# Passing quarter totals and the carry of a lane scan between partitions: small TensorE products or ScalarE copies

## The chip, the cores and the metric

One Trainium2 chip, one core of it. The kernel is one program; its five compute engines are named as in the profile: PE (TensorE, with PEld for its weight loads), DVE (VectorE), ACT (ScalarE), POOL (GpSimd) and SP (SyncE). Data lies in SBUF, which has 128 partitions, and PE writes to eight PSUM banks, here called d0, d1, d2, sc0, sc1, tr0, tr1 and yp. The metric is the time of one execution on the device, in microseconds; lower is better.

## What is computed

A gated linear scan with complex gates (4 batches, 8 heads, 768 tokens, width 48) gives x of 3072 tokens by 384 columns, and a layer pair with squared ReLU follows. Cut to what matters:

```python
mag = np.sqrt(a_re * a_re + a_im * a_im)
scale = np.minimum(mag, 0.999) / (mag + 1e-06)
a_re_n, a_im_n = (a_re * scale, a_im * scale)
for t in range(S):                     # per batch and head, state 48 x 48, complex
    new_re = ar * S_re - ai * S_im     # ar, ai: gate of token t, one per row
    new_im = ar * S_im + ai * S_re
    S_re, S_im = (new_re + outer(k_t, v_t), new_im)
    y[t] = q_t @ S_re
x = y.transpose(0, 2, 1, 3).reshape(3072, 384)
out = np.maximum(x @ w_in, 0) ** 2 @ w_out       # w_in 384 x 2048, w_out 2048 x 384
```

## The kernel before

**Units.** The 3072 tokens are worked off in six units of 512 (n = 0 to 5). A sequence has 768 tokens, so units 0 and 3 begin one ("fresh" is unit 3 in the code of the lane scan), units 1 and 4 have a border between two sequences in their middle ("cross"), and units 2 and 5 are plain. Within a unit the gates are turned into running products, so that the scan becomes matmuls with masks:

- the *chain* (`chain(n)`) takes roots, normalises the gates and forms their running complex product over the 512 tokens;
- `apply` multiplies q and k by it and by its inverse;
- the *pairs* (`pairs(n)`) work on eight pairs of heads: turn (line 1668), score (1689) with the mask on DVE (1692), keep (1717) with the state on DVE or ACT (1731, 1727), and mix (1748, 1752), whose sum ACT copies out of PSUM (1761) and DMAs carry into xT;
- the *dense* part is the layer pair: products of the first layer at line 1799, squared ReLU on ACT (1832, 1833), products of the second layer at line 1847 for unit 0 and at line 1910 for the rest; the last half unit has its own variant at line 2055. Between units, and in the first 130 us, weights are also split into 16-bit parts on ACT and DVE (lines 961 to 975).

**The lane scan.** In units 1 to 5 the running product is formed in `lanes()`. The 128 partitions are four quarters of 32, and within each quarter a lane holds a stretch of tokens. The running product is first formed inside the lanes on DVE (lines 1203 and 1215, with small copies on ACT at 1315). Then the quarters have to learn of each other. `times(dst, x, y, ...)` is one complex product of 128 x 24 numbers: one DVE instruction at line 1327 and two at line 1331. `qx` is the total of each quarter, made by `times` from the totals of two half quarters, h0 and h1. `exchange()` multiplies qx by `shifts`, a matrix 256 wide whose left half repeats the last 32 columns of the identity and whose right half is the identity. A window of it that is moved by 32, 64 or 96 columns gives qx shifted down by one, two or three quarters; where a quarter has no predecessor, it gets the value of the last quarter of qx, which is preset to 1. The results s1, s2, s3 lie in a bank tr0 or tr1. A plain unit then forms few2 = s2 * s3 (one operand is first copied from PSUM at line 1353), car = car * s1 and E0 = car * few2: what all lanes before this quarter have multiplied up to. Cross units need s1 alone.

**The carry.** `ce` is a unit's total at its end, needed by the next unit as `car`. `carry()` copies it from the last quarter to all four by one more product with `shifts` (line 1429) into a tr bank and one ACT copy out of it (line 1431). In cross units only the lower half is used, and POOL presets the upper half of car to 1 (times a scale, SCALE). Unit 1 uses another matrix for this, made by POOL at line 1426, since unit 0 leaves ce in a different layout (four ACT copies at line 1291).

**What sets the order.** All steps are entered in a list by `Plan.add` with engine, estimated duration, dependencies and a rank; `Plan.order()` then simulates the engines and picks the ready step with the lowest rank. `SHIFTS` adds numbers to the ranks of single steps, by their place in the list. `GROUP` is how long (in us) a narrow PE step (score or mix) is held back while another narrow one is about to get ready, so that they stand together. Engines then work off their instructions strictly in the emitted order, and DMAs stand in the queues of the engine that issues them (SP, ACT, POOL).

Of the kernel before, what the change touches and what calls it, by code (L numbers as in the profile page):

```python
# [16 lines left out]
ALU = mybir.AluOpType  # L17
# [464 lines left out]
class Plan:  # L482
# [13 lines left out]
    SHIFTS = {  # L496
        -2392.0: (2058,),
        -1993.0: (2427,),
        -1403.0: (2178,),
        -1100.0: (1860,),  # L500
        -1002.0: (1861,),
        -985.0: (1659,),
        -602.0: (1652,),
        -601.0: (1813,),
        -512.0: (1012,),
        -500.0: (1820,),
        -409.0: (1017,),
        -404.0: (1801,),
        -401.0: (1807, 1815,),
        -301.0: (2275,),  # L510
        -209.0: (541,),
        -202.0: (793, 795, 815, 821, 2276,),
        -197.0: (1818,),
        -104.0: (341,),
        -100.0: (range(109, 112), range(113, 116), 166, 229, 361, 432, 475, range(521, 523), 686,
            837, 940, 949, 982, 1397, 1403, range(1627, 1630), range(1762, 1764), 1806,
            range(1821, 1824), range(1827, 1829), range(2095, 2097), range(2098, 2100),
            range(2101, 2103), range(2104, 2106), 2116, 2163, 2165, 2236, range(2277, 2279),
            2431, 2562, 2581,),
        1.0: (2416, range(2434, 2436), 2444,),  # L520
        100.0: (27, 210, 234, 269, 290, 294, range(296, 298), 304, 306, 314, 327, 329, 386, 395,
            406, 425, 430, 434, 443, 449, 466, 473, 497, range(507, 509), 549, range(568, 570),
            582, 584, 587, 590, range(663, 665), 716, 720, 735, 738, 742, 789, 852, 891, 915,
            920, 925, 944, 961, 1129, range(1180, 1182), 1183, 1247, 1316, 1373, 1385, 1570,
            1719, 1732, 1784, 1798, 1819, 2161, 2174, 2222, 2362, 2382, 2386, 2394, 2437, 2440,
            2443, 2534, 2548, 2623, 2631, 2638, 2654,),
        198.0: (287,),
        202.0: (339,),
        203.0: (2114,),
        294.0: (1273,),  # L530
        297.0: (363,),
        299.0: (289, 808,),
        300.0: (1583,),
        306.0: (1824, 2085,),
        393.0: (585,),
        400.0: (787,),
        410.0: (1696,),
        429.0: (683,),
        496.0: (465,),
        504.0: (832,),  # L540
        506.0: (810,),
        508.0: (514,),
        509.0: (1694,),
        605.0: (535,),
        733.0: (682,),
        796.0: (2355,),
        807.0: (1699,),
        808.0: (1700,),
        906.0: (702,),
        907.0: (731, 737,),  # L550
        908.0: (1693,),
        1001.0: (751,),
        1008.0: (1697,),
        1010.0: (451,),
        1203.0: (753,),
        1317.0: (2536,),
        1320.0: (2567,),
        1505.0: (2031,),
        1515.0: (2591,),
        1614.0: (2600,),  # L560
        1734.0: (421,),
        1997.0: (537,),
        2341.0: (888,),
        2646.0: (894,),
        2969.0: (412,),
        3572.0: (409,),
        3772.0: (408,),
        3776.0: (413,),
        5321.0: (402,),
        9116.0: (36,),  # L570
        9619.0: (414,),
        10027.0: (31,),
        10523.0: (39,),
        10527.0: (410,),
        11514.0: (407,),
    }

    def __init__(self):
# [138 lines left out]
def fast_path(ctx, tc, q, k, v, a_re, a_im, moe_w_in, moe_w_out, out, flag):  # L717
# [6 lines left out]
    C = 128  # L724
# [11 lines left out]
    SCALE = 2.0 ** 59  # L736
# [19 lines left out]
    dve, pool, act, sp = nc.vector, nc.gpsimd, nc.scalar, nc.sync  # L756
    pe = nc.tensor
# [5 lines left out]
    def sb(name, n, dtype=F32, rows=C):  # L763
        return const.tile([rows, n], dtype, name=name)
# [18 lines left out]
    ce, car, qx = [sb(name, 2 * NK).rearrange("p (r k) -> p r k", r=2)  # L783
                   for name in ("ce", "car", "qx")]
# [270 lines left out]
    def chain(n):  # L1055
# [164 lines left out]
        K = kk_(0)  # L1220
# [18 lines left out]
        def scan():  # L1239
# [49 lines left out]
            for x in range(4):  # L1289
                own = slice(32 * x, 32 * x + 32)  # L1290
                step("ACT", 0.13, [("ce0",), ("A", 0)], [("ce",)], lambda x=x, own=own: act.copy(
                    out=ce[own].rearrange("p r (m x) -> p r m x", x=4)[:, :, :, x],
                    in_=ce0[own]), late[0], group="ce")

        def back(j):
# [8 lines left out]
        def lanes():  # L1304
# [27 lines left out]
                             out=dst[0:rows, r], in0=g[:, 0, r], in1=g[:, 1, 1 - r], op=op), rk)  # L1332

            times(qx, h0, h1, i4k, [("qx",)], rows=C - 32)
            if cross:
                def apart():
                    dve.memset(qx[32:64, 0], 1.0)
                    dve.memset(qx[32:64, 1], 0.0)
                step("DVE", 0.14, [], [("qx",)], apart, ahead)
            b = trs[take("tr", 2)]  # L1340
            s1, s2, s3 = [bank[b][:, j * 2 * NK:(j + 1) * 2 * NK].rearrange(
                "p (r k) -> p r k", r=2) for j in range(3)]

            def exchange():
                for j, o in enumerate((s1, s2, s3)[:1 if cross else 3]):
                    x0 = C - 32 * (j + 1)
                    pe.matmul(o, lhsT=shifts[:, x0:x0 + C], rhs=qx, start=True, stop=True)
            step("PE", 0.12 * (1 if cross else 3), [("qx",)], [(b,)], exchange, ahead)
            E0 = tx[:, :, 0:NK]
            two2, few2 = [KC[0][:, i:i + 2 * NK].rearrange("p (r k) -> p r k", r=2)  # L1350
                          for i in (64, 96)]
            if not cross:
                step("DVE", 0.1, [(b,)], [("ev", 0)], lambda: dve.tensor_scalar(
                    out=two2, in0=s2, scalar1=SCALE if fresh else 1.0, scalar2=None,
                    op0=ALU.mult), ahead)
            if cross:
                times(E0, car, s1, [(b,), ("car",)], [("tx", 0)])
            elif fresh:
                times(few2, two2, s3, [(b,), ("ev", 0)], [("ev",)])
                times(E0, s1, few2, [(b,), ("ev",)], [("tx", 0)])  # L1360
            else:
                times(few2, two2, s3, [(b,), ("ev", 0)], [("ev",)])
                times(car, car, s1, [(b,), ("car",)], [("car",)])
                times(E0, car, few2, [("car",), ("ev",)], [("tx", 0)])
            times(tx[:, :, NK:2 * NK], h0, E0, i4k + [("tx", 0)], [("tx", 1)])
            X = [("tx", 0), ("tx", 1)]
# [36 lines left out]
                times(ce, h1, tx[:, :, NK:2 * NK], i4k + X, [("ce",)], at=yts[0][:, 384:512], own="H", rk=late[1])  # L1403

        def carry():
            if fresh:
                return
            b = trs[take("tr", 2)]
            ps = bank[b][:, 0:2 * NK].rearrange("p (r k) -> p r k", r=2)
            rows = C // 2 if cross else C  # L1410

            def go():
                if cross:
                    pool.memset(car[C // 2:C, 0], SCALE)
                    pool.memset(car[C // 2:C, 1], 0.0)
            if cross:
                step("POOL", 0.2, [], [("car",)], go, ahead)

            by = shifts[:, 0:C]
            if n == 1:  # L1420
                by = KC[0][:, 1152:1152 + C]

                def same():
                    for x in range(4):
                        own = slice(32 * x, 32 * x + 32)
                        pool.tensor_copy(out=by[own].rearrange("p (b c) -> p b c", c=32),
                                         in_=ident[own, own].unsqueeze(1).to_broadcast([32, 4, 32]))
                step("POOL", 1.2, [], K, same, ahead)
            step("PE", 0.12, [("ce",)] + K * (n == 1), [(b,)], lambda: pe.matmul(
                ps, lhsT=by, rhs=ce, start=True, stop=True), ahead)  # L1430
            step("ACT", 0.15, [(b,)], [("car",)], lambda: act.copy(
                out=car[0:rows], in_=ps[0:rows]), ahead)

        if n:
            carry()
# [163 lines left out]
    def take(kind, n):  # L1599
        s = slot[kind]  # L1600
        slot[kind] = s + 1
        return s % n
# [615 lines left out]
```

## Time and profile before

| | |
|---|---|
| median of 3 runs | 663.99 us (663.62 to 665.3) |
| profiled execution, its own time | 663.7 us |
| its span, first to last instruction | 661.6 us |
| granted TensorE clock, mean | 0.990 |
| PE busy | 617.8 us (93%), 4424 records |
| PEld busy | 552.2 us (83%) |
| DVE busy | 589.1 us (89%) |
| ACT busy | 341.5 us (52%) |
| POOL busy | 120.6 us (18%) |
| chain that ended last, by engine | PE 70%, DVE 18%, DMA 6%, ACT 3% |

The profiled execution took 0.3 us less than the median, and 2.1 us of its own time lie outside its span. Each float32 matmul of the program shows as two PE records. Busy times of PE are modelled ends of a pipelined engine, so the start of one record against the start of the next tells more than the sum of durations.

### The profile page before, as it was taken

How to read it: one execution, taken by the hardware profiler on the slowest of the kernel's cores; microseconds unless marked ns; L12 is line 12 of the kernel's file. 1: busy time of each engine (PE TensorE's matmuls, PEld its weight loads, DVE VectorE, ACT ScalarE, POOL GpSimd, SP SyncE). 2: the span in 40 equal slices, each digit the busy share in tenths (PEclk: the TensorE clock that was granted, in tenths of full speed). 3: DMA queues.
4: the chain of work that ended last, by engine and by line, in shares of the span. 5: the costliest groups of instructions: out<-in, count | busy, mean ns of one | idle time of the engine just before them, and what ended most of it. 6: DMA issues, size and time to landing. Idle time of an engine off the chain costs nothing.

```text
span 661.6 us, 12065 instructions
## 1 busy us (share of the span) xinstructions
PE 617.8 (93%) x4424; PEld 552.2 (83%) x4424; DVE 589.1 (89%) x1196; ACT 341.5 (52%) x608; POOL 120.6 (18%) x208
## 2 busy tenths in 40 slices
PE   0468899999999999999999999999999999999996
PEld 0356887687679988999989999989989999988996
DVE  7999999899998999998979898989998997449982
ACT  7759979769626245438254447254446532035400
POOL 7402140221100032040121040111030130032100
PEclk9979999999999999999999999999999999999999
DMA  7963676024620056452056562056470063368541
GB/s 225 311 228 73 144 223 184 23 67 133 153 82 1 1 125 157 125 157 37 10 142 165 129 136 45 19 118 174 114 177 0 13 141 95 73 195 277 196 162 29
DMA packets 55269, 80.35 MB, mean 121 GB/s; under 512 B 11393, under 2 KB 37921, under 8 KB 55201
## 3 DMA queue, kind: packets, MB, share of 16 engines
q0 software_dynamic: 15424, 42.12, 22.5%
q1 hardware_dynamic: 35168, 31.93, 19.0%
q10 hardware_dynamic: 4608, 5.44, 3.2%
q8 instruction: 37, 0.61, 0.4%
q14 instruction: 32, 0.25, 0.1%
HBM read 48.76 MB, written 4.72 MB: 81 GB/s over the span
## 4 chain that ended last, share of the span: by engine, by line
PE 70%; DVE 18%; DMA 6%; ACT 3%; issue 2%; ACTq 0%; POOL 0%; DVEq 0%; SPq 0%
PE d L1910 25%; PE d L1799 24%; PE sc L1689 3%; PE yp L1748 3%; DVE f L1489 3%; PE d L1847 3%; DVE f L1554 3%; PE tr L1717 2%; DMA w<-in_moe_w_in_dram 2%; PE yp L1752 2%; PE d L2055 2%; PE tr L2055 2%; DVE aq L1642 1%; PE sc L2055 1%; DVE aq L1506 1%
## 5 line engine op out<-in xcount | busy, mean ns | idle before, releaser
L1799 PE MATMUL d<-xT,w 128*128 128x256 f32 x888 | 200.2, 381 | 0.8 <-DMA xT<-yt 0.5
L1799 PEld LDWEIGHTS d<-xT,w 128*128 128x128 f32 x888 | 166.5, 190 | 23.6 <-ACT g L1832 0.7
L1910 PE MATMUL d<-T,g 128*128 128x192 f32 x576 | 100.2, 329 | 0.0
L1910 PEld LDWEIGHTS d<-T,g 128*128 128x128 f32 x576 | 93.7, 190 | 1.5 <-issue 0.9
L1832 ACT ACTIVATE g<-d 128x512 f32<-128x512 f32 x74 | 44.1, 596 | 77.6 <-PE d L1799 64.6
L1865 POOL DMA_DIRECT2D out_dram<-ot x40 | 25.5, 642 | 277.7 <-DVE ot L1935 223.7
L1910 PE MATMUL d<-w,g 128*128 128x192 f32 x432 | 75.8, 328 | 0.3 <-ACT g L1833 0.3
L1910 PEld LDWEIGHTS d<-w,g 128*128 128x128 f32 x432 | 70.7, 190 | 1.5 <-ACT g L1833 0.6
L1590 POOL DMA_DIRECT2D KC<-f x60 | 32.4, 552 | 121.9 <-DVE f L1554 94.4
L1926 DVE TENSOR_TENSOR g<-g 128x512 f32<-128x512 f32 x72 | 48.5, 688 | 6.4 <-ACT g L1833 3.0
L1833 ACT ACTIVATE g<-g 128x512 f32<-128x512 f32 x80 | 50.5, 631 | 2.5
L1489 DVE TENSOR_TENSOR f<-aq,xn 128x384 f32<-128x384 f32 (+1 forms) x72 | 47.5, 686 | 0.0
L1847 PE MATMUL d<-w,g 128*128 128x384 f32 x128 | 44.2, 491 | 0.0
L1642 DVE STREAM_TRANSPOSE aq<-f 128x384 f32<-128x384 f32 (+1 forms) x51 | 42.1, 902 | 0.2
L1520 ACT ACTIVATE f<-aq 128x768 f32<-128x768 f32 (+1 forms) x16 | 17.3, 1081 | 43.7 <-DVE aq L1506 36.1
L1689 PEld LDWEIGHTS sc<-QT 96*64 96x64 f32 x736 | 33.5, 137 | 5.4 <-ACT QT L1672 2.0
L1689 PE MATMUL sc<-QT 96*64 96x128 f32 (+1 forms) x736 | 35.8, 249 | 1.9 <-DVE A L1692 0.8
L1128 DVE TENSOR_TENSOR f<-aq 128x384 f32<-128x384 f32 x72 | 37.1, 553 | 0.5
L1847 PEld LDWEIGHTS d<-w,g 128*128 128x128 f32 x128 | 23.6, 190 | 13.7 <-issue 0.2
L1935 DVE TENSOR_TENSOR ot<-ot,d 128x192 f32<-128x192 f32 x70 | 23.6, 350 | 10.3 <-PE d L1910 9.7
L1692 DVE TENSOR_TENSOR A<-sc,mask 128x512 f32<-128x512 f32 x45 | 29.6, 683 | 3.0 <-PE sc L1689 3.0
L1748 PE MATMUL yp<-A,v 128*48 128x128 f32 x312 | 29.0, 276 | 0.0
(315 smaller groups left out, 1104.5 us busy)
## 6 DMA issues: line engine op xcount, KB each, us to landing
QT<-aq SPq DMA_DIRECT2D x136, 64.0 KB, 2.1
f<-in_moe_w_in_dram POOLq DMA_DIRECT2D x8, 768.0 KB, 6.8
f<-in_moe_w_out_dram POOLq DMA_DIRECT2D x8, 768.0 KB, 5.3
QT<-aq ACTq DMA_DIRECT2D x68, 64.0 KB, 2.4
KC<-f POOLq DMA_DIRECT2D x40, 96.0 KB, 3.3
out_dram<-ot POOLq DMA_DIRECT2D x40, 96.0 KB, 3.6
xT<-yt SPq DMA_DIRECT2D x34, 96.0 KB, 2.6
T<-in_moe_w_out_dram POOLq DMA_DIRECT2D x4, 768.0 KB, 11.6
```

Source lines behind the costliest of these rows:

```text
L1128: lambda c=c, j=j: dve.tensor_tensor(out=f[:, j], in0=a[:, :, :, c - 1], in1=a[:, j, :, c].unsqueeze(1).to_broadcast([C, 2, HH, D]), op=AL ...
L1489: lambda j=j, r=r: dve.tensor_tensor(out=f4[:, j, r], in0=a[:, r], in1=over(j), op=ALU.mult), rk)
L1642: lambda src=src, dst=dst: dve.transpose(out=dst, in_=src), rank)
L1689: pe.matmul(sa[p0:p0 + CH, j, t0:], lhsT=T[:, j, 1, h, t0:t0 + CH], rhs=T[:, j, 0, h, t0:], start=True, stop=True)
L1748: pe.matmul(ps[64 * h:64 * h + D, j - js[0]], lhsT=v5[:, j, 2 * i + h], rhs=aa[h][:, j], start=True, stop=at[j] is None)
L1799: pe.matmul(ps, lhsT=w1[:, f // FP, m, ts(f % FP, C)], rhs=xT[:, n % 2, m, ts(grp, G)], start=(m == 0), stop=(m == NM - 1))
L1832: act.activation(out=o, in_=ps, func=AF.Relu)
L1833: act.activation(out=o, in_=o, func=AF.Square)
L1847: pe.matmul(ps, lhsT=gt[:, f % 2, ts(i, C)], rhs=w2[:, f], start=(f == 0), stop=(f == NF - 1))
L1910: pe.matmul(bank[b][:, 0:DH], lhsT=gsets[x][h][:, j - HW * h, r], rhs=w(j), start=first and j == 0, stop=last and j == NT - 1)
L1926: lambda: dve.tensor_tensor(out=g[:, :, o], in0=g[:, :, x0], in1=g[:, :, x1], op=op),
L2055: pe.matmul(ps[:, jj], lhsT=u[:, ts(jj, C)], rhs=v_, start=i == 0, stop=i == len(terms) - 1)
```

## The change

1. `exchange()`, its products and its bank go. In their place ACT copies quarters of qx into three SBUF tiles s1, s2, s3, shifted by 32, 64 or 96 partitions: two copies in a cross unit, five in each other unit. The quarters without a predecessor are preset to 1 and 0 once by POOL. DVE's copy out of PSUM (line 1353) and its two memsets of qx in cross units go too.
2. `carry()` has no product either: ACT copies the last quarter of ce to the quarters of car, four copies in units 2 and 5, two in units 1 and 4, none in unit 3. POOL presets what is left of car, in unit 3 all of it; unit 3 then also multiplies car by s1, which it did not before (three more DVE instructions). In cross units POOL also presets one quarter of s1. Unit 0 puts its four parts of ce into the last quarter, so that unit 1 needs no matrix of its own.
3. `shifts` shrinks to its right half, `ident`.
4. GROUP goes from 8 to 4, and the table SHIFTS is replaced as a whole, so that steps change places on every engine.

Counted over the program: 15 products less on PE (11 of exchange, 4 of the carry, 30 records), 31 small copies more on ACT and 4 copies out of PSUM less, 7 small instructions less and 3 more on DVE, some small presets more and fewer on POOL.

```diff
-    SETTLED, GROUP = 90.0, 8
+    SETTLED, GROUP = 90.0, 4
...
     SHIFTS = {
-        -2392.0: (2058,),
...
+        -4734.0: (468,),
...
-    shifts = sb("shifts", 2 * C)
-    ident = shifts[:, C:2 * C]
+    ident = sb("ident", C)
...
-    pool.tensor_copy(out=shifts[:, 0:C].rearrange("p (b c) -> p b c", c=32),
-                     in_=ident[:, C - 32:C].unsqueeze(1).to_broadcast([C, 4, 32]))
-    pool.memset(ce, 0.0)
-    pool.memset(qx[:, 0], 1.0)
-    pool.memset(qx[:, 1], 0.0)
+    for t in sx:
+        pool.memset(t[:, 0], 1.0)
+        pool.memset(t[:, 1], 0.0)
...
             times(qx, h0, h1, i4k, [("qx",)], rows=C - 32)
+            for j in range(1 if cross else 3):
+                for lo in (0, 64) if cross else (0, 32, 64) if j == 0 else (0,):
+                    hi = lo + (64 if j == 1 else 32)
+                    up = slice(lo + 32 * (j + 1), hi + 32 * (j + 1))
+                    step("ACT", 0.13, [("qx",)], [("sx", j)], lambda j=j, lo=lo, hi=hi, up=up: act.copy(
+                        out=sx[j][up], in_=qx[lo:hi]), ahead, group=(n, "sx"))
...
-            b = trs[take("tr", 2)]
-            s1, s2, s3 = [bank[b][:, j * 2 * NK:(j + 1) * 2 * NK].rearrange(
-                "p (r k) -> p r k", r=2) for j in range(3)]
-
-            def exchange():
-                for j, o in enumerate((s1, s2, s3)[:1 if cross else 3]):
-                    x0 = C - 32 * (j + 1)
-                    pe.matmul(o, lhsT=shifts[:, x0:x0 + C], rhs=qx, start=True, stop=True)
-            step("PE", 0.12 * (1 if cross else 3), [("qx",)], [(b,)], exchange, ahead)
...
-            if not cross:
-                step("DVE", 0.1, [(b,)], [("ev", 0)], lambda: dve.tensor_scalar(
-                    out=two2, in0=s2, scalar1=SCALE if fresh else 1.0, scalar2=None,
-                    op0=ALU.mult), ahead)
             if cross:
-                times(E0, car, s1, [(b,), ("car",)], [("tx", 0)])
-            elif fresh:
-                times(few2, two2, s3, [(b,), ("ev", 0)], [("ev",)])
-                times(E0, s1, few2, [(b,), ("ev",)], [("tx", 0)])
+                times(E0, car, sx[0], [("sx", 0), ("car",)], [("tx", 0)])
             else:
-                times(few2, two2, s3, [(b,), ("ev", 0)], [("ev",)])
-                times(car, car, s1, [(b,), ("car",)], [("car",)])
+                times(few2, sx[1], sx[2], [("sx", 1), ("sx", 2)], [("ev",)])
+                times(car, car, sx[0], [("sx", 0), ("car",)], [("car",)])
                 times(E0, car, few2, [("car",), ("ev",)], [("tx", 0)])
...
         def carry():
-            if fresh:
-                return
-            b = trs[take("tr", 2)]
...
-            step("PE", 0.12, [("ce",)] + K * (n == 1), [(b,)], lambda: pe.matmul(
-                ps, lhsT=by, rhs=ce, start=True, stop=True), ahead)
-            step("ACT", 0.15, [(b,)], [("car",)], lambda: act.copy(
-                out=car[0:rows], in_=ps[0:rows]), ahead)
+            rows = 0 if fresh else C // 2 if cross else C
+            if rows < C:
+                def start():
+                    pool.memset(car[rows:C, 0], SCALE)
+                    pool.memset(car[rows:C, 1], 0.0)
+                    if cross:
+                        pool.memset(sx[0][C // 2:C // 2 + 32, 0], 1.0)
+                        pool.memset(sx[0][C // 2:C // 2 + 32, 1], 0.0)
+                step("POOL", 0.4, [], [("car",), ("sx", 0)], start, ahead)
+            for b in range(rows // 32):
+                step("ACT", 0.13, [("ce",)], [("car",)], lambda b=b: act.copy(
+                    out=car[32 * b:32 * b + 32], in_=ce[C - 32:C]), ahead, group=(n, "car"))
```

The places where the order moves under the prediction's steps follow. In the rows a name stands with the number of its buffer; line numbers are those of each kernel's own file, so that 1799 before is 1784 after, 1692 is 1677, 1327 and 1331 are 1343 and 1347, 1832 and 1833 are 1817 and 1818, 968, 972 and 975 are 984, 988 and 991, and 1731 is 1716.

PE before, at the hand-over of unit 2's lane scan, where the first layer of an earlier unit runs:

```order
L1799 MATMUL d0_109<-xT_93,w1_66 128x256 x6
L1799 MATMUL d1_110<-xT_93,w1_66 128x256 x3
L1347 MATMUL tr1_115<-qx_83,shifts_97 128x24 x3
L1799 MATMUL d1_110<-xT_93,w1_66 128x256 x3
L1799 MATMUL sc1_113<-xT_93,w1_66 128x256 x4
```

PE after, at the same place:

```order
L1784 MATMUL sc1_116<-xT_96,w1_66 128x256 x4
L1784 MATMUL d0_112<-xT_96,w1_66 128x256 x6
L1784 MATMUL d1_113<-xT_96,w1_66 128x256 x6
L1784 MATMUL sc0_115<-xT_96,w1_66 128x256 x4
L1784 MATMUL yp_119<-xT_96,w1_66 128x256 x4
```

The three products of qx are gone, and the two halves of the tile d1 stand together.

DVE before, at the hand-over of unit 1 (qx made, preset for the border, then the first use of the shifted totals):

```order
L1327 TENSOR_TENSOR KC0_76<-yt0_91 96x48
L1331 TENSOR_TENSOR qx_83<-KC0_76 96x12 x2
L1337 MEMSET qx_83 32x12
L1338 MEMSET qx_83 32x12
L975 ISA w2_67<-T_72,w2_67 128x1536
L1327 TENSOR_TENSOR KC0_76<-car_82,tr1_115 128x48
```

DVE after, at the same place:

```order
L1343 TENSOR_TENSOR KC0_76<-yt0_94 96x48
L1347 TENSOR_TENSOR qx_83<-KC0_76 96x12 x2
L1343 TENSOR_TENSOR KC0_76<-car_82,s1_84 128x48
L1347 TENSOR_TENSOR tx_80<-KC0_76 128x12 x2
L1343 TENSOR_TENSOR KC0_76<-yt0_94,tx_80 128x48
```

The joining of weight parts that stood between qx and its first use is no longer there; the first reader of the copies comes directly behind qx.

ACT after, at the same hand-over (977 and 982 prepare parts of w_out, 1331 is a small copy inside the lanes, 1355 is the new copy):

```order
L977 ACTIVATE T_72<-T_72 128x768
L1331 COPY yt0_94<-e_79 128x96 x2
L982 ACTIVATE T_72<-T_72 128x768
L1355 COPY s1_84<-qx_83 32x24 x2
L1376 COPY KC0_76<-tx_80 128x2x12
```

The copies of qx stand behind one long preparation of weights (982, which is 966 before).

DVE before, around the last masks of unit 0 (1692), the last scores ahead of the first layer:

```order
L1692 TENSOR_TENSOR A1_88<-sc1_113,mask_98 128x512
L1692 TENSOR_TENSOR A0_87<-sc0_112,mask_98 128x512
L975 ISA w1_66<-g_96,w1_66 128x1536
L968 TENSOR_SCALAR w1_66<-T_72 128x768
L1731 TENSOR_TENSOR St1_90<-tr1_115,St1_90 96x96 x2
L968 TENSOR_SCALAR w1_66<-g_96 128x768
L972 SCALAR_TENSOR_TENSOR w1_66<-g_96,w1_66 128x768
L1692 TENSOR_TENSOR A0_87<-sc0_112,mask_98 128x512
L1692 TENSOR_TENSOR A1_88<-sc1_113,mask_98 128x512
```

DVE after, at the same place:

```order
L988 SCALAR_TENSOR_TENSOR w1_66<-g_99,w1_66 128x768
L1100 TENSOR_TENSOR f0_70<-f0_70 128x768
L991 ISA w1_66<-g_99,w1_66 128x1536
L984 TENSOR_SCALAR w1_66<-w2_67 128x768
L991 ISA w1_66<-w2_67,w1_66 128x1536
L1677 TENSOR_TENSOR A0_90<-sc0_115,mask_101 128x512
L1716 TENSOR_TENSOR St1_93<-tr1_118,St1_93 96x96
L1677 TENSOR_TENSOR A1_91<-sc1_116,mask_101 128x512
```

Other splittings of w_in stand between the masks now, and over the whole of unit 0 three instructions of line 968 that stood ahead of the last mask stand behind it.

More of the change, by code (lines that the diff above doesn't have):

```diff
@@ L515 @@
[L515 to L526, printed above, removed]
@@ L568 @@
[L568 to L575, printed above, removed]
+        -4734.0: (468,),
+        -4118.0: (582,),
+        -4010.0: (1085,),
+        -3812.0: (1083,),
+        -3809.0: (583,),
+        -3735.0: (471,),
+        -3719.0: (580,),
+        -2621.0: (593,),
+        -2610.0: (591,),
+        -2298.0: (816,),
+        -2202.0: (814,),
+        -1816.0: (544,),
@@ new lines @@
+        -1624.0: (1008,),
+        -1419.0: (463,),
+        -1219.0: (1012,),
+        -1207.0: (320,),
+        -1008.0: (946,),
+        -997.0: (466,),
+        -904.0: (1643, 1646,),
+        -898.0: (1133,),
+        -897.0: (592,),
+        -894.0: (562,),
+        -806.0: (1623,),
+        -804.0: (1614, 1620,),
+        -704.0: (1649,),
+        -703.0: (1132,),
+        -698.0: (469,),
+        -697.0: (417,),
+        -678.0: (292,),
+        -605.0: (458,),
+        -603.0: (1617,),
@@ new lines @@
+        107.0: (1720,),
+        194.72: (9,),
+        195.02: (11,),
+        206.0: (1689,),
+        296.0: (2124,),
+        397.0: (854,),
+        398.0: (933,),
+        402.0: (985,),
+        409.0: (1230,),
+        500.0: (930,),
+        591.0: (2157,),
+        603.0: (1419,),
+        609.0: (2377,),
+        610.0: (864,),
+        710.0: (871,),
+        804.0: (1188,),
+        906.0: (1890,),
+        908.0: (856,),
+        1015.0: (870,),
+        1200.0: (1167,),
+        1204.0: (1429,),
@@ L576 @@
+        1406.0: (867,),
+        1605.0: (1185,),
+        1917.0: (438,),
+        2115.0: (868,),
+        2592.0: (2185,),
+        4190.0: (402,),
+        4199.0: (1360,),
+        4296.0: (410,),
+        4487.0: (426,),
+        4892.0: (431,),
+        5820.0: (446,),
+        6733.0: (419,),
+        6932.0: (430,),
+        7038.0: (442,),
     }
@@ L782, in fast_path @@
     tx = sb("tx", 4 * NK).rearrange("p (r g) -> p r g", r=2)
-    ce, car, qx = [sb(name, 2 * NK).rearrange("p (r k) -> p r k", r=2)
-                   for name in ("ce", "car", "qx")]
+    ce, car, qx, *sx = [sb(name, 2 * NK).rearrange("p (r k) -> p r k", r=2)
+                        for name in ("ce", "car", "qx", "s1", "s2", "s3")]
     xn = sb("xn", 2 * DM).rearrange("p (r n) -> p r n", r=2)
@@ L1291, in scan @@
                 step("ACT", 0.13, [("ce0",), ("A", 0)], [("ce",)], lambda x=x, own=own: act.copy(
-                    out=ce[own].rearrange("p r (m x) -> p r m x", x=4)[:, :, :, x],
+                    out=ce[C - 32:C].rearrange("p r (m x) -> p r m x", x=4)[:, :, :, x],
                     in_=ce0[own]), late[0], group="ce")
```

117 lines of the change are left out of this document (34 added, 83 removed).

## The prediction

> **What bounds the kernel now.** I read first the page's shares, then the engine sums by stretch, then PE's waits from the first dense products to the end, and last the neighbourhood of each product that goes. The shares and PE's row of tenths:
>
> ```profile
> PE 617.8 (93%) x4424; PEld 552.2 (83%) x4424; DVE 589.1 (89%) x1196; ACT 341.5 (52%) x608; POOL 120.6 (18%) x208
> PE   0468899999999999999999999999999999999996
> ```
>
> PE and DVE are both near full, so the shares alone don't decide. The sums by stretch (length, then busy time and count of PE, PEld, DVE, ACT, POOL, then clock, DMA share, GB/s):
>
> ```profile
> core 0: us, PE busy (x) PEld busy (x) DVE busy (x) ACT busy (x) POOL busy (x), PEclk, DMA share, GB/s
> 52.00:86.00 34.00, 29.13 (x382) 25.81 (x381) 33.45 (x67) 30.33 (x50) 5.98 (x12) 1.00 0.49 112
> 86.00:260.00 174.00, 173.26 (x1094) 142.65 (x1092) 165.78 (x356) 110.09 (x197) 34.15 (x56) 1.00 0.40 105
> 260.00:656.00 396.00, 394.70 (x2855) 367.15 (x2854) 342.73 (x661) 165.78 (x292) 59.26 (x91) 1.00 0.44 115
> ```
>
> From 86 us on PE lacks 0.74 and 1.30 us; DVE has 8 and 53 us to spare there. PE's waits from 86 to 656 us (total, times, longest):
>
> ```profile
> PE tr L2055 <- DMA xT<-yt: 1.0, 1, 1.0
> PE tr L1429 <- DVE St L1731: 0.5, 1, 0.5
> PE d L1910 <- ACT g L1833: 0.3, 1, 0.3
> PE d L1799 <- ACT g L1832: 0.3, 1, 0.3
> ```
>
> Four waits in 570 us, 2.1 us together. So here PE streams, and what is taken out of its stream should shorten the time by its place in the stream. Ahead of 86 us it is the other way: DVE is busy 33.45 of 34 us, and PE waits for it. What is in doubt is whether a stream that waits for nothing also has work ready that may move up.
>
> **The products that go.** PE records overlap, so I price a product by the start of its first record to the start of PE's next work:
>
> ```profile
> 203.67 2.11 PE L1799 MATMUL d<-xT,w 128*128 128x256 f32 x9
> 205.61 0.74 PE L1347 MATMUL tr<-qx,shifts 128*128 128x24 f32 x6
> 206.20 1.54 PE L1799 MATMUL d<-xT,w 128*128 128x256 f32 x6
> ...
> 402.91 0.30 PE L1347 MATMUL tr<-qx,shifts 128*128 128x24 f32 x2
> 403.05 4.13 PE L1799 MATMUL d<-xT,w 128*128 128x256 f32 x18
> ```
>
> ```profile
> 179.49 0.40 PE L1429 MATMUL tr<-ce,shifts 128*128 128x24 f32 x2 [0.45 <-DVE St L1731]
> 179.74 1.54 PE L1847 MATMUL d<-w,g 128*128 128x384 f32 x4
> ...
> 372.51 0.40 PE L1429 MATMUL tr<-ce,shifts 128*128 128x24 f32 x2
> 372.76 1.55 PE L1910 MATMUL d<-T,g 128*128 128x192 f32 x8
> ```
>
> Three products of qx take 206.20 - 205.61 = 0.59 us (units 2, 3, 5), one takes 0.14 (units 1, 4), a carry 0.25 (four of them). 3 x 0.59 + 2 x 0.14 + 4 x 0.25 = 3.05 us. The carry at 179.49 also stands 0.45 us for its bank, which DVE's state sums still hold; with no bank wanted this goes. What is late next there: the product at 179.74 has its inputs, since its neighbours of the same line ran just before the wait. Together **-3.5 us**; some carries show less than 0.25, so I book **-3.4**.
>
> **The turns between narrow and wide products.** GROUP 4 holds narrow steps back for less long. In the emitted order PE goes 36 times instead of 35 into the narrow ones. What the first narrow load costs:
>
> ```profile
> PEld sc L1689 <- issue: 2.0, 8, 0.3
> ```
>
> 0.25 us for one, and I take the way back as part of it: **+0.25**. Ends: 0, if the load is hidden behind the product before it, and 0.5 with a way back of the same size.
>
> **The copies on ACT.** 31 more, and four copies out of PSUM less:
>
> ```profile
> L1291 ACT COPY ce<-A 32x6 f32<-32x6 f32 x4 | 0.8, 195 | 0.0
> L1376 ACT COPY KC<-tx 128x24 f32<-128x24 f32 x5 | 1.0, 201 | 1.9 <-DVE tx L1331 1.9
> L1431 ACT COPY car<-tr 64x24 f32<-64x24 f32 (+1 forms) x4 | 0.7, 171 | 3.9 <-PE tr L1429 3.0 <-ACT yt L1761 0.9
> ```
>
> 31 x 0.20 - 4 x 0.17 = +5.5 us of ACT's 341.5. As throughput that costs nothing: ACT idles 64 us from 86 to 260 and 230 us from 260 to 656. If that cover failed it would cost the 5.5. [...]
>
> **The hand-over.** What can cost is latency: DVE's next instruction behind qx needs the copies, and they stand in ACT's queue. Today:
>
> ```profile
> 204.47 0.25 DVE L1331 TENSOR_TENSOR qx<-KC 96x12 f32<-96x12 f32 x2
> 206.39 0.18 DVE L1353 TENSOR_SCALAR KC<-tr 128x24 f32<-128x24 f32 x1 [1.67 <-PE tr L1347]
> ```
>
> Over all units DVE waits there for PE:
>
> ```profile
> DVE KC L1353 <- PE tr L1347: 3.4, 2, 1.8
> ...
> DVE KC L1327 <- PE tr L1347: 0.8, 1, 0.8
> ```
>
> That is 4.2 us, 1.67 of them in unit 2, because the products stand in PE's stream. PE does not wait for DVE at that place or behind it (no such row among the four waits). A plain unit's five copies take 5 x 0.2 = 1.0 us, of which the reader of s2 and s3 needs the first four, and before them one pair of ACT instructions may be in progress:
>
> ```profile
> L966 ACT ACTIVATE T<-T 128x768 f16<-128x768 int16 x5 | 9.7, 1941 | 0.0
> L1833 ACT ACTIVATE g<-g 128x512 f32<-128x512 f32 x80 | 50.5, 631 | 2.5
> ```
>
> So the new delay lies between 0.8 us (ACT free) and 0.8 + 2 x 0.63 = 2.1 (units 2 to 5), about today's 1.67. In unit 1 it is new: the order now has the weight preparation of 1.94 us right ahead of the copies, and the weight joining that filled DVE's time there has gone elsewhere, so DVE idles up to 1.94 + 2 x 0.2 = 2.3 us. Behind DVE's reader the whole chain of the next unit is queued. I book **0** for all five, since PE has a unit's dense work as stock. DVE's own work shrinks by 4 presets and 3 copies and grows by three instructions of unit 3 (about 0.2 us each): equal within 0.3 us, and booked at nothing, as are POOL's presets (18% busy).
>
> **The front.** PE's waits from 52 to 86 us, and then unit 0's last masks on DVE, the first dense product (from the chain of waits), and a kind of instruction that moves:
>
> ```profile
> PE d L1668 <- DVE f L1554: 2.5, 2, 1.9
> PE sc L1689 <- DVE A L1692: 0.8, 1, 0.8
> PE sc L1689 <- ACT yt L1761: 0.5, 1, 0.5
> PE d L1799 <- DMA xT<-yt: 0.5, 1, 0.5
> ```
>
> ```profile
> 81.64 1.28 DVE L1692 TENSOR_TENSOR A<-sc,mask 128x512 f32<-128x512 f32 x2
> ...
> 82.65 1.13 PE d L1799 x4
> ...
> L968 DVE TENSOR_SCALAR w<-T 128x768 uint32<-128x768 uint32 x5 | 2.7, 554 | 0.1
> ```
>
> In the new order three instructions of line 968 (0.55 us each, 1.7 us) that stood ahead of the last mask stand behind it, while some others moved ahead; by the sum of the instructions in the order DVE comes to that mask about 1.4 us earlier. That may not all reach PE, since the last rows of xT also wait for ACT and a DMA. I take half, **-0.7**. Ends: -3 (the four waits shown sum to 4.3, of which the change of order could remove most) and +1 (the two loads of k are now issued behind ten other loads, so unit 0's first q and k work could come late).
>
> **The sum.** -3.4 + 0.25 - 0.7 = -3.85. On the profiled execution, 663.7 - 3.85 = 659.85; its 2.1 us outside the span stay. The median is 0.3 us above it: **660.0 us**, 0.6% faster. 0.3% of the time, 2.0 us, is about what a measurement here tells from no change, so "same" reaches from 662.0 to 666.0.
>
> **Rivals.**
>
> *The front gives more.* If the new order removes 3 us of the front's waits, the time is 663.99 - 3.4 + 0.25 - 3 = 657.8; with the ends 656.5 to 658.8. For it: DVE is full there and the order was changed most there. Against it: DVE has the same work to do before the second unit, and what is put behind the mask must be done soon after.
>
> *DVE governs until 262 us.* The chain that ended last runs over DVE there and goes over to PE as follows:
>
> ```profile
> 261.91 0.64 ACT g L1833
> 262.59 1.24 PE d L1910 x6
> ```
>
> If what ends at 262 us is set by DVE, products ahead of it are covered, and those behind it count: units 3, 4 and 5 with 0.59 + 0.14 + 0.59 and two carries of 0.25, 1.82 in all. 663.99 - 1.82 = 662.2, same. Against it: from 86 to 260 us DVE has 8 us idle, and PE has next to none. [...]
>
> *The hand-over is late.* On the other side: in each unit the copies wait for the ACT instruction or pair ahead of them and DVE idles through it. With 1.94 in unit 1 and 1.26 in the four others plus the copies (0.4, 1.0, 1.0, 0.4, 1.0) this is 7.0 + 3.8 = 10.8 us. Today's 4.2 us go, so DVE comes 6.6 us later by the end. If the stock of dense work doesn't cover it, and all becomes PE's, the time is 663.99 - 3.4 + 6.6 = 667.2, slower. It decides from 3.4 + 2.0 = 5.4 us of lateness on. For it: DVE has only 8 us idle until 260. Against it: 53 us idle behind 260, and today's 1.67 us cost PE nothing. A shuffled order that is worse in some stage ends on the same side, at about the same size.
>
> **Chances.** Forecast 0.52 (658.8 to 662.0), more in front 0.17 (656.5 to 658.8), same by cover 0.19 (662.0 to 664), late hand-over 0.12 (above 666). Faster is the first two together, 0.69. The range leaves out the late hand-over and the tail under 656.5, and takes in most of the covered cases: 656.5 to 663.3. The forecast's own range is 658.8 to 662.0.
>
> **What would show it.** No product of lines 1347 and 1429 in PE's rows, and PE's busy time lower by some 3 us; the stretch from the first dense product to the end of PE's stream shorter by as much, and no new wait in PE's list of more than a few tenths. First dense product at about 82 instead of 82.65 us. DVE's waits for the new copies (where line 1353 waited for PE) under 2.3 us each, and no PE wait for DVE behind them. The forecast is wrong if PE's list from 86 us on has new waits for DVE, ACT or xT of together over 1.5 us; if the time is the same and PE's waits grew by the 3.4 us, work wasn't ready; if the first dense product comes at 84 us or later, the front's loads or squares did it.

## The result and the profile after

| | before | after |
|---|---|---|
| median | 664.47 us (663.62 to 665.3) | 658.86 us (657.96 to 659.93) |
| ratio, 95% interval | | 0.9916 (0.9895 to 0.9938) |
| a second measurement, ratio and interval | 664.95 us | 660.35 us (659.63 to 663.07), 0.9931 (0.9918 to 0.9943) |
| span of the profiled execution | 661.6 us | 658.2 us |

The change makes the kernel faster by 0.84% in the first and 0.69% in the second measurement. The profiled execution of after (659.93 us) is the longest of its four, that of before (663.7) near the shortest of its own, so that the two traces show 3.4 us of the 4.6 to 5.6 between the medians. The page of after:

```profile
PE 616.7 (94%) x4394; PEld 551.1 (84%) x4394; DVE 586.2 (89%) x1192; ACT 347.9 (53%) x635; POOL 118.9 (18%) x212
...
PE 82%; DVE 8%; DMA 5%; ACT 2%; issue 1%; POOL 1%; SPq 0%; ACTq 0%; DVEq 0%
```

PE has 30 records less, ACT 6.4 us more; the shares of the chain that ended last go from DVE (18% to 8%) to PE (70% to 82%). The sums by stretch, with the columns of the table in the prediction (length, busy time and records of PE, PEld, DVE, ACT and POOL, granted clock, DMA share, GB/s); the last stretch ends where PE's stream ends, at 652.6 us instead of 656.0:

```profile
52.00:86.00 34.00, 31.14 (x390) 27.89 (x388) 33.77 (x69) 30.68 (x52) 4.35 (x8) 1.00 0.47 114
86.00:260.00 174.00, 172.42 (x1092) 142.31 (x1090) 167.43 (x359) 111.37 (x204) 34.02 (x56) 1.00 0.41 106
260.00:652.60 392.60, 391.50 (x2819) 362.99 (x2818) 339.07 (x657) 170.35 (x309) 59.49 (x95) 1.00 0.44 115
```

From 52 to 86 us PE is busy 2.0 us more than before; behind, it streams as before, and is done 3.4 us earlier. PE's waits from 86 us to the end of its work:

```profile
PE d L1784 <- DMA xT<-yt: 1.3, 1, 1.3
PE d L1784 <- issue: 0.9, 1, 0.9
PE tr L1653 <- ACT St L1712: 0.2, 1, 0.2
```

The bank wait of 0.5 at the carry is gone, as is the wait for xT that before had in unit 5; two others have come. What replaced the products at the hand-over, first DVE's waits over the whole kernel, then unit 2 on ACT and DVE:

```profile
DVE KC L1343 <- ACT s L1355: 5.5, 5, 1.4
...
203.48 1.10 ACT L1355 COPY s<-qx 32x24 f32<-32x24 f32 x5
...
204.38 0.21 DVE L1343 TENSOR_TENSOR KC<-s,s 128x48 f32<-128x48 f32 x1 [1.21 <-ACT s L1355]
```

Five copies take 1.10 us, and DVE waits 1.21 us there instead of 1.67; over all five units 5.5 instead of 4.2.

**Where the time went, place by place.** To compare two traces whose order differs, I gave every kind of PE record (by its shape) its median distance to the next start, and asked at which time each kernel had done the same sum of PE work (without the products in question). A distance above this median is called a gap below. This is the lead over the profiled execution of before, in us (minus is ahead), at before's time of that work:

```
at (before)        97    141    183    223    306    408    489    570    592    653
after            -0.5   -0.6   -1.5   -1.8   -3.1   -3.4   -2.2   -2.5   -3.7   -3.7
products, priced -0.2   -0.4   -1.1   -1.7   -2.3   -2.7   -2.9   -3.5   -3.5   -3.5
```

The second row adds up the prices of the prediction in order of time (0.25 of the carry at 85 us, then 0.14, 0.25 with the 0.45 of its bank, 0.59, 0.59, 0.25, 0.14, 0.25, 0.59). The lead grows where the products stood, from the first one on. It falls at 482 us by about 1.1, where PE waits 0.9 us for nothing that the profile shows, and comes back at 585 us, where before waits for xT.

### The profile page after: what moved, and what is told of

It is laid out like the page before. It is cut to its first block, busy times and chain, and to the rows that moved or that the text cites. A ratio compares the mean times of both kernels' runs of the same rounds, so it can differ in the third digit from the quotient of the medians.

```text
span 658.2 us, 12025 instructions
## 1 busy us (share of the span) xinstructions
PE 616.7 (94%) x4394; PEld 551.1 (84%) x4394; DVE 586.2 (89%) x1192; ACT 347.9 (53%) x635; POOL 118.9 (18%) x212
## 4 chain that ended last, share of the span: by engine, by line
PE 82%; DVE 8%; DMA 5%; ACT 2%; issue 1%; POOL 1%; SPq 0%; ACTq 0%; DVEq 0%
PE d L1895 28%; PE d L1784 27%; PE sc L1674 4%; PE d L1832 4%; DMA w<-in_moe_w_in_dram 3%; PE yp L1733 3%; PE tr L1702 3%; PE yp L1737 2%; DVE f L1474 2%; PE d L2040 2%; PE tr L2040 2%; PE sc L1784 2%; DVE f L1539 2%; PE sc L2040 1%; DMA aq<-in_a_im_dram 1%
## 5 line engine op out<-in xcount | busy, mean ns | idle before, releaser
L1746 ACT COPY yt<-yp 112x512 f32<-112x512 f32 (+1 forms) x20 | 11.7, 584 | 33.7 <-PE yp L1737 33.7
```

## The experiments

To move one thing at a time, all kernels below issue their steps by a fixed list instead of the planner, except the changed kernel itself, the one with tripled products and the two with extra ACT instructions, where the planner's order stays as it was. All ratios are against the kernel before, run beside them on the same chip.

### Copies and order apart

```diff
-        order = self.order()
+    ORDER = [ ... ]                      # old order, copies where the products stood
```

The changed kernel again:

> The changed kernel once more, as the yardstick beside the others: 658 to 660 us, about 0.9915 of the kernel before. My theory is that the 15 small products and the bank wait of one of them stood in a stream of PE that waits for nothing (worth 3.4 us), and that the rest of the gain, 0.3 us in the profiled pair and up to 2 us in the medians, comes from the new order.

Copies in the old order:

> The ACT copies instead of the products, in the order of the kernel before: every other instruction of PE, DVE, ACT, POOL and SP stands where it stood, the copies stand where the products stood in the program. Theory (products lie in PE's stream): 3.0 to 3.5 us less than before, 661.2 us or 0.995. Rival one (DVE governs until 262 us, only later products count): 1.8 us less, 662.7 us or 0.9973. Rival two (the hand-over through ACT's queue makes DVE late where the order is not made for it): same or slower than before.

Products in the new order:

```diff
-  step("ACT", 0.13, [("qx",)], [("sx", j)], ... act.copy(out=sx[j][up], in_=qx[lo:hi]) ...)
+  step("ACT", 0.13, [("qx",)], [("sx", j)], exchange ...)   # products into tr0, a free bank here
```

> The new order with products instead of copies, in 14 of the 15 places (the carry of unit 1 stays with copies); each product is put in 0.7 us behind its copies' place, DVE's copy out of PSUM and its presets are back. Theory: 2.8 us (3 x 0.59 + 2 x 0.14 + 3 x 0.25) above the changed kernel, about 661.7 us, with no other change of PE's waits. If copies matter only for the order, the same as the changed kernel; if the order were what won, near it too.

The new front with the old rest:

> Copies, with the new order for what is planned ahead of 100 us and the old order behind. Theory: the new front brings what the two traces show at equal PE work at 96 us, 0.3 us beyond the products, so 0.3 us less than the copies in the old order, up to 2 us if the wait of 1.3 us for xT that the new trace has at 87.7 us goes in other executions; 659.5 to 661.2 us. If the rest of the new order is what wins, the same as the copies in the old order.

And, run later, the old front with the new rest:

> The changed kernel with the old order for what was planned ahead of 100 us, and the new order behind. Theory: the part behind 90 us brings 2.6 to 3.2 us by the two traces (time at equal PE work, -0.5 to -3.7 and +2.3 to -0.3), most of it products; so 661.3 to 661.9 us, 0.995 to 0.996, without the spread of the changed kernel. If the new front is what brought the rest, it stays at the copies in the old order (0.9963) or above; if the new front costs in most executions, it is faster than the changed kernel.

| | products | copies |
|---|---|---|
| old order | 1 | 0.9963 (0.9949 to 0.9977) |
| new order | 1.002 (1.0005 to 1.0034) | 0.9931 (0.9918 to 0.9943) |
| new front, old rest | | 0.9956 (0.9942 to 0.997) |
| old front, new rest | | 1.0003 (0.9988 to 1.0017) |

The copies alone bring 2.5 us (1.5 to 3.4 by the interval). That rules out a hand-over that eats it all; it does not tell 1.8 us (products behind 262 us alone) from the 3.0 to 3.5 that were expected. What part was given back stands in PE's waits from 86 to 656 us of the copies in the old order:

```profile
PE tr L2120 <- DMA xT<-yt: 1.1, 1, 1.1
PE d L1975 <- DVE ot L2000: 0.7, 2, 0.4
PE d L1864 <- ACT g L1897: 0.5, 1, 0.5
PE d L1975 <- ACT g L1898: 0.2, 1, 0.2
PE d L1864 <- DVE ot L2000: 0.2, 1, 0.2
```

DVE's sums of the second layer (ot) and ACT's squares (g) now come 0.2 to 0.5 us after PE wants them, 16 to 56 us behind a product that went. Gaps of more than 0.2 us in PE's stream sum to 3.9 us behind 100 us, against 2.7 before and 1.8 after. With copies, the new order is 2.1 us faster than the old one (0.9963 less 0.9931, times 665; the intervals don't meet), and the traces read as follows: it has work ready where the old one has not. Which part of the order does it, GROUP or SHIFTS, was not taken apart.

The other cell is not clean. It came to 665.61 us, where 661.7 was expected: the products, put in by hand, make DVE wait longer for them in the new order,

```profile
DVE KC L1442 <- PE tr L1440: 7.8, 3, 2.8
...
DVE KC L1423 <- PE tr L1440: 3.8, 2, 2.3
```

11.6 us instead of 5.5. Between the ends of PE's work in this trace and in that of the result lie 5.0 us: about 2.8 are products by their prices, and gaps of more than 0.2 us sum to 6.2 us from 78 us on, against 3.8. This run shows that the new order alone is no gain with products so placed; how a planner would have placed them was not tried.

Neither mixed order keeps the gain of the new one. The old front with the new rest loses all (665.16 us, where 661.3 to 661.9 was expected), and PE's waits from 86 us on say where:

```profile
PE d L1909 <- ACT g L1894: 1.7, 1, 1.7
PE d L1861 <- issue: 1.0, 1, 1.0
PE d L1861 <- ACT g L1894: 0.7, 1, 0.7
PE d L1909 <- DVE w L1068: 0.7, 1, 0.7
```

They stand at 109 to 128 us, just behind the seam at 100 us. In the first of them ACT works on a splitting of weights (line 1059) and on a pass over q (line 1520) ahead of the squared ReLU that PE wants, and in the last DVE's joining of weights is late; that the old front left this work in another state than the new rest counts on is argued, not shown. By equal PE work this kernel is 4.4 us behind at 141 us and 1.1 at the end: behind the seam the new rest gains 3.3, in the changed kernel 3.1. The new front with the old rest was expected at 659.5 to 661.2 us and came to 662.08: by equal PE work it is 0.8 us ahead of before at 97 us and 0.3 behind at 141, so it too loses its lead at the seam. A mixture has a seam that neither order was planned for, so these two runs do not price the front or the rest of an order by itself.

### The price of a product, from the other side

```diff
-                    pe.matmul(o, lhsT=shifts[:, x0:x0 + C], rhs=qx, start=True, stop=True)
+                    for _ in range(3):
+                        pe.matmul(o, lhsT=shifts[:, x0:x0 + C], rhs=qx, start=True, stop=True)
...
-            step("PE", 0.12, [("ce",)] + K * (n == 1), [(b,)], lambda: pe.matmul(
-                ps, lhsT=by, rhs=ce, start=True, stop=True), ahead)
+            step("PE", 0.12, [("ce",)] + K * (n == 1), [(b,)], lambda: [pe.matmul(
+                ps, lhsT=by, rhs=ce, start=True, stop=True) for _ in range(3)], ahead)
```

> The kernel before, with each of the 15 products issued three times into the same bank: 30 products (60 records) more, nothing else moved. Theory (each lies in PE's stream at its price in the trace): 2 x 3.05 = 6.1 us more than before, ratio 1.009. Rival, only products behind 262 us count: 2 x 1.82 = 3.6 us, 1.0055. Rival, small products fit into gaps between weight loads: under 1 us, 1.001.

Measured: 1.0086 (1.0066 to 1.0106), 5.7 us for 30 products, or 0.19 us each, where 6.1 was expected. The rival of small products that fit into gaps between weight loads (under 1 us) is out, and 3.6 us (products behind 262 us alone) lies under the interval, which begins at 4.4 us. PE still waits for little behind 86 us, while DVE's waits at the hand-over grew:

```profile
PE tr L2056 <- DMA xT<-yt: 0.5, 1, 0.5
PE d L1911 <- ACT g L1834: 0.3, 1, 0.3
PE d L1800 <- ACT g L1833: 0.2, 1, 0.2
PE tr L1430 <- DVE St L1732: 0.2, 1, 0.2
...
DVE KC L1354 <- PE tr L1348: 7.8, 3, 3.5
```

### What a late hand-over costs

Extra ACT instructions that read qx (0.84 us each in their row) were put ahead of the first copy, three or one in each unit:

```diff
+                            for _ in range(3):
+                                act.activation(out=junk[0:C - 32]..., func=AF.Square, in_=qx[0:C - 32]...)
                         act.copy(out=sx[j][up], in_=qx[lo:hi])
```

> The changed kernel, with three extra ACT instructions ahead of the copies in each of the five units; each reads qx (96 x 768 elements, some 0.84 us by the rows of line 1458), so that the copies and DVE behind them come about 2.5 us later, 12.6 us over all. Theory: PE has a unit's dense work as stock, at most 1 us above the changed kernel, 0.993. Rival: lateness of DVE goes on to PE; products in the new order had 6.1 us more of DVE waits there than the changed kernel and 2.4 us more of gaps in PE's stream, 0.4 us for each, so some 5 us more, ratio 0.9995 or slower.

> As with three extra ACT instructions ahead of the copies, but with one in each unit: the copies come 0.84 us later in each of five units, 4.2 us in all. Three cost 13.6 us for 13.2 us more of DVE's waits. If lateness is passed on from the first one on (no stock left in the new order), 4.2 us above the changed kernel, 664.5 us, ratio 0.9995. If the stock covers the first microseconds and the price starts later, under 1.5 us, 661.5 us.

And the wait was taken away, by DVE making the copies itself, in both orders:

```diff
-  ... act.copy(out=sx[j][up], in_=qx[lo:hi]), ahead, group=(n, "sx"))
+  ... dve.tensor_copy(out=sx[j][up], in_=qx[lo:hi]), ahead, group=(n, "sx"))
```

> The changed kernel with the 19 copies of qx made by DVE itself right behind qx, ACT's copies gone. By DVE's small rows (two of line 1331 in 0.25 us) a copy takes some 0.13 us, 2.4 us in all, against 5.5 us of waits for ACT today. Theory (lateness of DVE is passed on): up to 3 us less than the changed kernel, 657.3 us, 0.9885. Rival (three extra instructions were dear because they blocked ACT's other work, not because DVE came late): same as the changed kernel, 0.993.

> DVE's copies in the old order. In the old order the ACT copies made DVE wait 5.0 us, and PE's gaps behind 100 us summed to 3.9 us against 2.7 before. If those gaps came from the hand-over, DVE's copies bring up to 2.5 us beyond the ACT copies in the old order, 659.7 us, 0.992; if they come from the order of the other work (DVE's sums of the second layer, ACT's squares), the same, 0.9963.

| copies of qx | DVE's waits and copies there | ratio, interval |
|---|---|---|
| by DVE | no wait, 3.2 us of copies | 0.9933 (0.9917 to 0.9948) |
| by ACT (the changed kernel) | 5.5 us | 0.9931 (0.9918 to 0.9943) |
| one extra instruction each | 9.9 us | 0.9987 (0.9977 to 0.9997) |
| three extra each | 18.7 us | 1.0143 (1.012 to 1.0165) |
| by DVE, old order | no wait, 3.2 us of copies | 0.9975 (0.9963 to 0.9986) |

DVE's waits for the copies and PE's waits, first with one, then with three extra instructions:

```profile
PE d L1904 <- DVE g L1920: 1.8, 3, 0.8
...
DVE KC L1343 <- ACT s L1364: 9.9, 5, 2.2
```

```profile
PE d L1904 <- DVE g L1920: 7.0, 4, 2.6
PE d L1793 <- ACT ot L1846: 2.1, 1, 2.1
...
DVE KC L1343 <- ACT s L1364: 18.7, 5, 4.0
```

This speaks for an edge near the 5.5 us of the changed kernel. Below it, nothing is gained that stands out of the noise: DVE's own copies, 170 ns each,

```profile
L1432 DVE COPY s<-qx 32x24 f32<-32x24 f32 (+1 forms) x19 | 3.2, 170 | 0.4
```

take 2.3 us off the lateness and leave the time where it is in the new order (within some 1.3 us by the two intervals), and in the old one by its interval. Nothing was tried below 3.2 us. The up to 3 us expected of them was a miss. Above 5.5 us, one extra instruction costs 3.7 us (some 1 us either way by the intervals) for 4.4 us of lateness, 0.85 for each, and three cost 14.1 us for 13.2: the ratios less that of the changed kernel, 0.0056 and 0.0212, times 665 us. In the profiled execution with three, a part of the 14.1 us is the clock: it was granted at half speed in two stretches of 3.4 us (last section), worth up to 1.7 us each, and without them some 0.8 us are left for each microsecond.

Not all of it comes by way of DVE. By what ended them last, PE's waits from 86 us on are 1.8 us for DVE and 1.3 for ACT with one extra instruction, 7.0 and 3.6 with three, against 0 and 0.2 in the changed kernel. ACT's own work waits behind the same extra instructions (2.1 us at line 1793, at 130 us). The waits for DVE's sums (line 1920) end 2 to 17 us behind the hand-overs of units 2, 3, 4 and 5, at 223, 316 and 507 us with one extra instruction and at 226, 321, 418 and 515 us with three.

### The front and the clock

```diff
+            if n == 466:
+                self.idle()
...
+    def idle():
+        for _ in range(6):
+            pe.matmul(bank["tr0"][:, 0:C], lhsT=ident, rhs=ident, start=True, stop=True)
```

Step 466 is the product that waits for the last rows of xT.

> The changed kernel with six products of the identity by itself (128 x 128, result not used) put on PE right ahead of the place where it waits for the last rows of xT at 86 us; they take some 1.3 us of the wait. Theory: with them the gap stays under 1.5 us and the granted clock stays at 1.00 from 85 to 95 us, while without them a wait of 2.2 us lowered it to 0.88 and 0.78 there and seven products behind it took 0.21 us longer each; so the slow third of the changed kernel's executions goes, median 0 to 1.5 us less, 0.991 to 0.993. Rival: clock and wait don't matter, same median and spread as the changed kernel, or 0.5 us more where xT lands early.

> DVE's copies, and six products of the identity on PE ahead of the wait for xT. Theory: both together, 0.3 us and a narrower spread on top of DVE's copies: 657 us, 0.988. This is the version that should beat both kernels.

In the changed kernel the first dense product starts at 80.48 us instead of 82.65, and then PE waits for xT. The same place in the profiled executions of the first and of the second measurement, the second with the sums of the two stretches around it:

```profile
80.48 1.10 PE L1784 MATMUL d<-xT,w 128*128 128x256 f32 x4
...
87.70 2.83 PE L1784 MATMUL d<-xT,w 128*128 128x256 f32 x12 [1.34 <-DMA xT<-yt]
90.37 1.89 PE L1784 MATMUL yp<-xT,w 128*128 128x256 f32 x8
```

```profile
88.92 4.45 PE L1784 MATMUL d<-xT,w 128*128 128x256 f32 x12 [2.21 <-DMA xT<-yt]
93.20 1.89 PE L1784 MATMUL yp<-xT,w 128*128 128x256 f32 x8
...
85.00:90.00 5.00, 2.79 (x11) 2.08 (x11) 4.93 (x6) 3.36 (x3) 0.41 (x2) 0.88 0.53 134
90.00:95.00 5.00, 5.00 (x20) 4.22 (x19) 4.97 (x9) 1.31 (x3) 5.00 (x7) 0.78 1.01 264
```

After a wait of 1.34 us the twelve records take 2.67 us (90.37 - 87.70) at a granted clock of 1.00 from 85 to 95 us, after one of 2.21 us 4.28 (93.20 - 88.92) at 0.88 and 0.78. The second of these executions took 663.07 us, the first 659.93; of the 3.1 us between them, 2.8 are there by equal PE work at 97 us, right behind this place. With six products in the wait, the clock in these stretches is 1.00:

```profile
85.00:90.00 5.00, 5.00 (x31) 4.56 (x30) 4.93 (x6) 3.31 (x3) 2.06 (x4) 1.00 0.85 205
90.00:95.00 5.00, 5.00 (x25) 4.41 (x24) 4.93 (x9) 4.32 (x7) 4.63 (x6) 1.00 1.00 263
```

The time is 660.07 us (659.34 to 660.51), 0.9926 (0.9908 to 0.9944): the spread is 1.2 us instead of 3.4 (2.0 in the first measurement), the median the same within its interval. Together with DVE's copies it measured 0.9944 (0.9929 to 0.9959), 659.0 to 661.72 us, so the narrower spread did not show again, and no version here beats the changed kernel. The dip as such is shown; that it makes the longest executions is shown for the one that was profiled.

## Why the prediction was right, point by point

- **The products, -3.4.** Right as a mechanism: PE's stream pays for each product, ahead of 262 us and behind it, 0.19 us each when added. As a term it holds only with the new order (-3.7 in the table above, grown where the products stood); in the old order 2.5 us came, since 1.2 us more of gaps opened. The prediction named this doubt (whether work is ready that may move up) and priced it at nothing. The order then brought 2.1 us where the prediction booked 0.45 for it (-0.7 and +0.25): taken apart this way, one term is 0.9 us too large and the other 1.7 too small, and that the sum holds is in part luck.
- **The turns, +0.25.** Too small to be told from other terms.
- **The copies on ACT.** ACT's busy time rose by 6.4 us, 5.5 expected, at no cost as throughput. The row of a copy,

```profile
L1355 ACT COPY s<-qx 32x24 f32<-32x24 f32 (+1 forms) x19 | 4.0, 208 | 2.3 <-DVE qx L1347 2.0
```

208 ns, is near the 195 and 201 of the two rows of before from which 0.20 was taken. With the 4.0 us of these copies taken off ACT (DVE's copies, 0.9933 against 0.9931) the time stayed.
- **The hand-over, 0.** The size was right, the reason was not. The waits of units 2 to 5 (1.2 to 1.4 us) lie within the 0.8 to 2.1 forecast, and unit 1's, up to 2.3 by forecast, is 0.5. But "PE has a unit's dense work as stock" is wrong: the stock ends at about the lateness that the kernel has, and 4.4 us more cost 3.7. What was booked at nothing stood at the edge, so that this term held by luck.
- **The front, -0.7.** DVE did reach the last pair of masks 1.3 us earlier (1.4 expected), and the first dense product starts 2.17 us earlier (0.65 expected). PE then waits 1.34 us for the last rows of xT, so 0.5 is left at 97 us, 0.2 of it the first carry's. Taking half because ACT and a DMA come in between was the right reason: what took the rest is a wait for a DMA. That in the profiled execution of the second measurement this wait was 2.21 us, with the clock at 0.88 and 0.78 behind it, was not foreseen.
- **The sum.** 3.85 forecast; 3.4 between the profiled spans, 4.6 and 5.6 between the medians. The first median, 658.86 us, lies at the edge of the forecast's own range (658.8 to 662.0), the second inside it. The terms say little on the rest: unit 5's wait for xT (1.0 us) went, a wait of 0.9 us at 482 us came, and the executions differ by 2 us among themselves.
- **The rivals.** *DVE governs until 262 us* falls: the lead is 1.8 us at 223 us, the chain's share of DVE fell, and the products added in the other direction cost more than those behind 262 us can. *The hand-over is late* had its price about right (each microsecond counts) and its amount wrong: 1.3 us more of waits than before, not 6.6. It counted a pair of ACT instructions ahead of the copies in full, but by the time qx is done part of the pair is over (0.96 of 1.26 us in unit 2). *The front gives more* is half true: the medians of the first measurement need it, the traces do not show it.
- **The signs.** Not all that the prediction named as signs came. PE's busy time fell by 1.1 us, not some 3; behind 86 us it fell by 4.0, since ten further records had moved ahead of 86 us. From the first dense product to the end of PE's stream it is 1.6 us less, not 3.4, because that product starts early and PE then waits; from 97 us on it is 3.2. And the new waits for xT and ACT behind 86 us sum to 1.56 us (1.34 and 0.23), just over the 1.5 at which the prediction called itself wrong. Together with the 0.9 us at 482 us they are 2.5 us, where the waits before were 2.1; the mark looked at new waits alone, and old ones of the same size went.

## What to carry to other kernels

In a stream of PE that waited for 2.1 of 570 us, added products cost about their start-to-start distance (5.7 us, priced at 6.1), but taking products out did not pay in full where the next inputs were not ready sooner too: of 3.4 us booked, 2.5 came in the old order, and a reordering of other work collected the rest. Before a hand-over is booked at nothing, delay it by one instruction and see: here the cover that looked like 50 us of idle time on DVE was used up. And an order tuned as a whole cannot be judged by halves; front and rest apart gave 0 to 0.4% where both together gave 0.7%.

## What the runs showed of the hardware

Behind a PE wait of 2.21 us the granted clock fell to half for 3.4 us (worked out from 0.88 and 0.78 in two stretches of 5 us; half is the 0.50 that the trace of the first measurement shows from 33 to 42 us), and twelve of PE's records of 128x256 took 4.28 us instead of 2.67; behind a wait of 1.34 us at the same place the clock stayed at 1.00. The fall came twice more in the execution with three extra instructions on ACT, behind waits of 2.1 us (at 130 us) and 2.6 us (at 513 us), again for about 3.4 us each by the clocks in these stretches:

```profile
129.00:132.00 3.00, 0.95 (x4) 0.33 (x3) 1.84 (x11) 1.67 (x6) 1.71 (x4) 1.00 0.76 167
132.00:136.00 4.00, 4.00 (x12) 3.21 (x12) 3.90 (x11) 0.00 (x0) 1.28 (x2) 0.57 0.22 55
...
225.80:230.00 4.20, 4.07 (x23) 3.80 (x24) 4.17 (x11) 2.15 (x5) 0.00 (x0) 1.00 0.00 0
...
515.00:520.00 5.00, 4.74 (x20) 4.77 (x21) 4.11 (x16) 2.49 (x7) 0.00 (x0) 0.67 0.00 0
```

In the same execution the clock stayed at 1.00 behind a wait of 2.4 us that ended at 225.9 us (PE is busy 1.57 of the 3.80 us from 222 us on and 4.07 of the next 4.20), so the length of the wait alone does not decide. The copies of qx between partitions, 16 of 32 x 24 and three of 64 x 24, took 208 ns in the mean on ACT and 170 on DVE.
